# A Mamba-2 scan with a gated FFN on one Trainium2 core: the first chunk's scan in two units of 64 tokens, and the start-up in another order

## The chip, the core and the metric

The kernel runs on one core of a Trainium2 chip. The core has a matrix engine (TensorE, PE in the profile; PEld is its weight load), a vector engine (VectorE, DVE), an activation engine (ScalarE, ACT), a general engine (GpSimd, POOL) and a sequencer that issues transfers (SyncE, SP); each works through its own queue in order, and semaphores tie the queues together. Matrix products land in PSUM, everything else lies in SBUF, the inputs and the output in HBM. The metric is the device time of one execution in microseconds (us), the median of several runs; lower is better.

## The reference

Two parts are joined. The first is a state-space scan over four sequences, 8 heads, 768 tokens, 32 values a head and a state of 16; the second is an FFN of width 256 to 2048 to 256 on all 3072 tokens, with the gate h * cos(h). All data are fp32.

```python
log_a = np.log(np.clip(a, 1e-06, 1.0))
for c in range(nc):                        # the result does not depend on the chunk's length
    cum = np.cumsum(la, axis=-1)
    L = np.exp(cum[:, :, :, None] - cum[:, :, None, :]) * causal
    CB = np.einsum('bhin,bhjn->bhij', Cc, Bc)
    y_intra = np.einsum('bhij,bhjd->bhid', CB * L, xc)
    y_inter = np.einsum('bhin,bhnd->bhid', Cc, state) * np.exp(cum)[:, :, :, None]
    y[:, :, sl] = y_intra + y_inter
    Bx = np.einsum('bhjn,bhjd->bhjnd', Bc, xc) * decay_from_j[:, :, :, None, None]
    state = decay_full[:, :, None, None] * state + np.sum(Bx, axis=2)
# ... y as rows of tokens, heads side by side: x of (3072, 256)
h = x @ w_in
g = h * np.cos(h)
return g @ w_out
```

## The kernel before

The kernel cuts the 768 tokens into six chunks of 128 (NC = 6). A chunk's FFN is 16 steps (NF = 16); step n makes one PSUM bank of h (`first`), its cosine and gate, and two steps later adds to the output (`second`). The scan of chunk c + 1 is slipped in between the steps of chunk c. Only chunk 0 has no FFN before it to hide its scan behind. Its u is one of two halves of the tokens, and even and odd steps alternate between them:

```python
def turn_of(n):
    c, f = divmod(n, NF)
    return (f % 2, f // 2) if c == 0 else divmod(f, NJ)

def first(n):
    hp[n] = bank([P, TB], "hp", "h")           # two banks in turn
    for e in range(2):
        for k in range(KT):
            PE.matmul(to_[:, e], lhsT=w_in[:, k, fs], rhs=y[:, k, u], ...)
    ACT.activation(k, hp[n], AF.Copy, bias=0.25, scale=INV_2PI)
    V.scalar_tensor_tensor(out=w, in0=hp[n], scalar=INV_2PI, in1=k, ...)
```

Chunk 0's scan takes the four sequences one after the other, 128 tokens each. The decays between tokens j and i come from products of a: a is spread over partitions by a matmul (`spread_a`) and multiplied up by a running product on VectorE (`decays0`). The block from the second 64 tokens to the first 64 comes from another matmul (`cross`).

```python
def spread_a(b, tag):                          # 2 matmuls of 64x512
    for t in range(2):
        PE.matmul(ps[t * W:(t + 1) * W], lhsT=those[:, b:b + 1].to_broadcast([P, W]), rhs=a0s[:, t], ...)

def decays0(b):                                # one scan of 128x512, then GpSimd moves a half
    V.tensor_tensor_scan(out=l[:, 0]..., data0=spread.pop(b)..., data1=unit0..., ...)
    G.tensor_copy(out=l[W:P, 1], in_=l[W:P, 0])
    G.memset(l[W:P, 0], 0.0)

def turn(b, tag=None):                         # B and C of one sequence transposed, C cut in two
    for k in range(2):
        PE.transpose(tp[:, k], bc[:, k, heads(b)]..., ident)
    ...
def intra(b):                                  # g = C B^T, m = g * lam
    ...
def finish(b, tag, fills=0):                   # y = m x, and its copy to SBUF
    for h in range(H):
        PE.matmul(y[32 * q:32 * q + 32, t], lhsT=xr[:, b, h], rhs=m[:, :, h], ...)
    ACT.copy(out=yT[0][:, :, b * P:(b + 1) * P], in_=y[:, 0:2])
```

The weights of the FFN come in 16 pieces of 512 KB ("in" 0 to 7, "out" 0 to 7). They arrive as pairs of 32-bit words, and each piece is turned into fp32 by `grade` and `join`:

```python
def grade(which, i, later=False, n=1):
    ACT.activation(mags[e], high[e].bitcast(FP32), AF.Abs)
    G.tensor_scalar(out=mags[e], in0=mags[e], scalar1=MOST, scalar2=LEAST, ...)
    ACT.activation(lasts[e], low[e], AF.Copy, scale=2.0 ** -29)

def join(which, i):
    V.tensor_scalar(out=bits, in0=bits, scalar1=3, scalar2=0x3FFFFFFF, ...)
    V.scalar_tensor_tensor(out=bits, in0=high, scalar=0xC0000000, in1=bits, ...)
    G.tensor_tensor(out=dst.bitcast(U32), in0=bits, in1=last, op=ALU.add)
```

The start of the program, in the order in which each engine gets its instructions:

```python
fill(warm, 2)                                  # matmuls on ones, nobody reads them
spread_a(0, "h"); turn(0); spread_a(1, "h"); spread_a(2, "o"); spread_a(3, "h")
for b in range(NB):
    decays0(b)
turn(1, "h"); cross(0, "o"); intra(0); turn(2, "h"); cross(2, "o"); intra(1)
finish(0, "o"); grade("in", 0, n=2); intra(2); turn(3, "h"); finish(1, "o", 1)
# ... cut and la: all of a, clipped, written to HBM for the later chunks
join("in", 0); finish(2, "o"); intra(3)
grade("in", 1); rest = grade("out", 0, later=True); join("in", 1)
for n in range(NC * NF + LAG):
    first(n)
    if n == 0:
        first_scan()                           # finish(3), and the sums for the states
    # ... grade the next piece, gate(n), join, gated(n); from n = 2 on second(n - 2)
```

Of the kernel before, what the change touches and what calls it, by code (L numbers as in the profile page):

```python
# [25 lines left out]
def kernel(  # L26
# [10 lines left out]

# [54 lines left out]
    def load(c, seqs=(0, NB), only=(B, C, x)):  # L108
# [8 lines left out]
        for dst, src in ((bc[:, 0], B), (bc[:, 1], C), (xr, x))[::2 if c > 1 else 1]:  # L117
# [3 lines left out]
            halves = c > 0 and src is not C  # L121
# [9 lines left out]

    def by_blocks(c, u):
        return c > 1

    def load_blocks(c, u):


# [33 lines left out]
    a0 = const.tile([P, P], FP32, name="a0")  # L171
    a0z = const.tile([P, P], FP32, name="a0z")
    nc.sync.dma_start(out=a0[0:NB * H], in_=a[:, :, 0:P].rearrange("b h p -> (b h) p"))
    for r in (slice(NB * H, W), slice(W, P)):
        V.memset(a0[r], 1.0)
# [34 lines left out]

# [19 lines left out]
    def join(which, i):  # L230

        parts = held.pop((which, i), ())
        for e, (high, bits, last) in enumerate(parts):
# [12 lines left out]
    for b in range(NB):  # L248
        if b == NB - 1:
            fetch("in", 0)  # L250
        load(0, (b, b + 1))
    nc.sync.dma_start(
        out=a_in, in_=a.rearrange("(u b) h (c p) -> (b h c) u p", u=NU, p=P))
    for w in (("in", 1), ("out", 0), ("in", 2), ("out", 1), ("in", 3)):
        fetch(*w)
# [5 lines left out]
    V.memset(quarter, HALF_PI)  # L261


    unit = const.tile([P, HH * P + W], FP32, name="unit")
    G.tensor_copy(out=unit[:, 0:HH * P].rearrange("p (h i) -> p h i", h=HH),
                  in_=ident.unsqueeze(1).to_broadcast([P, HH, P]))


    ms = [scan.tile([P, 2 * H * W], FP32, tag=f"m{b}", bufs=1, name="m") for b in range(NB)]
    m_of = [t.rearrange("p (e h i) -> p e h i", e=2, h=H) for t in ms]  # L270
    m_at = [t.rearrange("p (h i) -> p h i", h=H) for t in ms]
    unit0, tos = m_of[NB - 1][:, 0], m_of[NB - 1][:, 1]
    for t in range(2):
        ts = slice(t * W, (t + 1) * W)
        V.tensor_copy(out=unit0[ts], in_=ident[ts, ts].unsqueeze(1).to_broadcast([W, H, W]))

    slot = const.tile([P, 2], FP32, name="slot")
# [7 lines left out]

    ACT.activation(const.tile([P, 1], FP32, name="sine"), quarter, AF.Sin)


    clip = dict(scalar1=1.0, scalar2=1e-6, op0=ALU.min, op1=ALU.max)
    G.tensor_scalar(out=a0z, in0=a0, **clip)  # L290
    G.memset(a0z[:, 0:P:W], 0.0)
    V.tensor_scalar(out=a0, in0=a0, **clip)


    to = const.tile([P, W], FP32, name="to")
    V.tensor_tensor_scan(out=to, data0=a0[:, W:P], data1=ones[:, 0:W], initial=1.0,
                         op0=ALU.mult, op1=ALU.mult)
    fro = const.tile([P, W], FP32, name="fro")
    V.memset(fro, 1.0)
    V.tensor_tensor_scan(out=fro[:, W - 2::-1], data0=a0[:, W - 1:0:-1],  # L300
                         data1=ones[:, 0:W - 1], initial=1.0, op0=ALU.mult, op1=ALU.mult)
    fros = const.tile([P, NB, W], FP32, name="fros")
    V.tensor_tensor(out=fros, in0=fro.unsqueeze(1).to_broadcast([P, NB, W]),
                    in1=those.unsqueeze(2).to_broadcast([P, NB, W]), op=ALU.mult)
    V.tensor_reduce(out=slot, in_=ident.rearrange("p (k t n) -> p t k n", t=2, n=N),
                    axis=mybir.AxisListType.XY, op=ALU.add)


    a0s = m_of[NB - 2]
    halves = a0z.rearrange("p (t i) -> p t i", t=2)  # L310
    for h in range(HH):
        ACT.activation(a0s[:, :, h], halves, AF.Copy, scale=mine[:, h:h + 1])
    for t in range(2):
        G.tensor_tensor(out=a0s[:, t, HH:H], in0=halves[:, t:t + 1].to_broadcast([P, HH, W]),
                        in1=mine[:, HH:H].unsqueeze(2).to_broadcast([P, HH, W]), op=ALU.mult)
    G.tensor_tensor(out=tos, in0=to.unsqueeze(1).to_broadcast([P, H, W]),
                    in1=mine.unsqueeze(2).to_broadcast([P, H, W]), op=ALU.mult)
# [6 lines left out]

    spread = {}

    def spread_a(b, tag):


        spread[b] = ps = bank([P, H, W], "a_ps", tag)  # L330
        for t in range(2):
            PE.matmul(ps[t * W:(t + 1) * W], lhsT=those[:, b:b + 1].to_broadcast([P, W]),
                      rhs=a0s[:, t], start=True, stop=True, tile_position=(0, t * W),
                      skip_group_check=True)

    def decays0(b):

        lam[0, b] = l = scan.tile([P, 2, H, W], FP32, tag="lam", bufs=4, name="lam")  # L340
        flat = "p h i -> p (h i)"
        V.tensor_tensor_scan(out=l[:, 0].rearrange(flat), data0=spread.pop(b).rearrange(flat),
                             data1=unit0.rearrange(flat), initial=0.0,
                             op0=ALU.mult, op1=ALU.add)
        G.tensor_copy(out=l[W:P, 1], in_=l[W:P, 0])
        G.memset(l[W:P, 0], 0.0)

    def cross(b, tag):

        ps = bank([P, H, W], "l_ps", tag)  # L350
        PE.matmul(ps, lhsT=fros[:, b:b + 2].rearrange("p b j -> p (b j)"), rhs=tos,
                  start=True, stop=True)
        for t in range(2):
            ACT.copy(out=lam[0, b + t][0:W, 1], in_=ps[t * W:(t + 1) * W])
            weigh(0, b + t)
# [31 lines left out]
    def turn(b, tag=None):  # L387
# [8 lines left out]
        for t in range(2):  # L396
            ACT.activation(cT[:, t], tp[:, 1], AF.Copy, scale=slot[:, t:t + 1])
# [517 lines left out]
```

## Time and profile before

| | before |
|---|---|
| time, median of 3 runs | 376.96 us (376.21 to 377.3) |
| span of the profiled execution | 374.9 us |
| first matmul of step 0 (hp, L578) | 17.81 us |
| first matmul of the second product (o, L637) | 25.71 us |
| one step of the FFN in chunk 0, hp and o | 3.46 us |
| last matmul ends | 371.2 us |

In the views, a line begins with a time from the start of the span, a length, the engine, the line of the kernel, the operation, and output <- inputs by their names; what stands in square brackets is the time for which the engine was idle just before, and who released it. A matmul in fp32 counts as two instructions (x8 for the four of one step). The granted clock of TensorE is 0.998 of full speed over the span. The two last microseconds after the last matmul are the last output's way to HBM.

### The profile page before, as it was taken

The numbers are of one execution on the slowest core, as the hardware profiler recorded it, in microseconds if no ns is written. First come the engines' busy times: TensorE is split into PE (matmuls) and PEld (weight loads), VectorE is DVE, ScalarE is ACT, GpSimd is POOL, SyncE is SP. The second block draws the span as 40 slices with busy tenths as digits, with TensorE's granted clock in tenths as the row PEclk, the third lists the DMA queues.
The fourth block names the chain that finished last, engine by engine and source line by source line (L and its number), as shares of the span: only waits on it lengthen the run. The fifth ranks groups of instructions, "written<-read, shape, count | busy, mean of one in ns | idle before, by whom it ended". The sixth has DMA issues, their size and how long they took to land.

```text
span 374.9 us, 8382 instructions
## 1 busy us (share of the span) xinstructions
PE 367.1 (98%) x3108; PEld 325.4 (87%) x3108; DVE 286.0 (76%) x478; ACT 176.0 (47%) x304; POOL 215.1 (57%) x335
## 2 busy tenths in 40 slices
PE   8999999999999999999999999999999999999996
PEld 3478888889899899999899998999999989999995
DVE  8879999889799957987767987766887872554543
ACT  3887666544344434344334445434444443443442
POOL 6767555589946346665354693353775344444451
PEclk9999999999999999999999999999999999999999
DMA  7989896514545741663322655121020000010011
GB/s 84 263 239 285 243 219 117 128 15 99 151 92 78 131 108 16 84 153 77 76 54 21 91 141 131 25 51 17 4 41 8 11 21 2 0 30 0 2 28 29
DMA packets 124424, 31.52 MB, mean 84 GB/s; under 512 B 93568, under 2 KB 120288, under 8 KB 124384
## 3 DMA queue, kind: packets, MB, share of 16 engines
q1 hardware_dynamic: 124224, 30.86, 38.4%
q8 instruction: 24, 0.39, 0.4%
q14 instruction: 16, 0.13, 0.1%
q10 hardware_dynamic: 160, 0.13, 0.1%
HBM read 27.64 MB, written 3.34 MB: 83 GB/s over the span
## 4 chain that ended last, share of the span: by engine, by line
PE 83%; SPq 5%; POOL 4%; DMA 3%; DVE 2%; issue 1%; ACT 1%; POOLq 0%; DVEq 0%; ACTq 0%
PE hp L578 40%; PE o L675 29%; PE o L637 7%; SPq L127 4%; PE y L516 3%; PE g L474 2%; DMA words<-in_moe_w_in_dram 1%; POOL words L613 1%; PE y L509 1%; POOL gd L619 1%; DMA bc<-in_B_dram 1%; DMA blocks<-in_C_dram 1%; POOL gd L622 1%; PE o L720 1%; PE s_ps L537 0%
## 5 line engine op out<-in xcount | busy, mean ns | idle before, releaser
L578 PE MATMUL hp<-yT,w_in 128*128 128x256 f32 x768 | 183.7, 382 | 1.9 <-DVE gT L594 1.4
L578 PEld LDWEIGHTS hp<-yT,w_in 128*128 128x128 f32 x768 | 139.4, 190 | 21.6 <-issue 2.0
L619 POOL TENSOR_TENSOR gd<-gT 128x256 f32<-128x256 f32 x79 | 59.2, 750 | 100.0 <-DVE gT L594 91.2
L589 ACT ACTIVATE w<-w,quarter 128x512 f32<-128x512 f32 x96 | 69.2, 721 | 76.8 <-DVE w L584 76.7
L582 ACT ACTIVATE k<-hp 128x512 int32<-128x512 f32 x96 | 57.2, 595 | 82.3 <-PE hp L578 82.0
L584 DVE SCALAR_TENSOR_TENSOR w<-hp,k 128x512 f32<-128x512 f32 x96 | 65.4, 681 | 37.3 <-ACT k L582 37.1
L594 DVE TENSOR_TENSOR gT<-hp,w 128x512 f32<-128x512 f32 x96 | 65.2, 679 | 34.6 <-ACT w L589 24.8
L675 PE MATMUL o<-words,gd 128*128 128x128 f32 x474 | 65.9, 275 | 0.0
L675 PEld LDWEIGHTS o<-words,gd 128*128 128x128 f32 x474 | 59.3, 192 | 0.1
L378 DVE TENSOR_TENSOR_SCAN lam<-arow,unit 128x512 f32<-128x512 f32 x40 | 57.0, 1426 | 0.0
L675 PEld LDWEIGHTS o<-w_out,gT 128*128 128x128 f32 x316 | 47.5, 191 | 4.0
L622 POOL TENSOR_TENSOR gd<-gT,gd 128x128 f32<-128x128 f32 x79 | 45.5, 577 | 6.2
L675 PE MATMUL o<-w_out,gT 128*128 128x128 f32 x316 | 48.0, 274 | 0.0
L621 POOL TENSOR_TENSOR gd<-gT,gd 128x128 f32<-128x128 f32 x79 | 44.2, 560 | 6.2
L495 DVE TENSOR_TENSOR m<-g,lam 128x256 f32<-128x256 f32 x80 | 30.9, 415 | 0.5
L637 PE MATMUL o<-w_out,gT 128*128 128x256 f32 x128 | 30.3, 380 | 0.4 <-POOL w_out L246 0.4
L675 PE MATMUL o<-w_out,gd 128*128 128x128 f32 x158 | 30.6, 275 | 0.0
L675 PE MATMUL o<-words,gT 128*128 128x128 f32 x158 | 30.6, 275 | 0.0
L637 PEld LDWEIGHTS o<-w_out,gT 128*128 128x128 f32 x128 | 24.2, 190 | 4.0 <-POOL w_out L246 0.8
L675 PEld LDWEIGHTS o<-words,gT 128*128 128x128 f32 x158 | 24.0, 192 | 0.0
L675 PEld LDWEIGHTS o<-w_out,gd 128*128 128x128 f32 x158 | 24.0, 192 | 0.0
L692 DVE TENSOR_TENSOR sum<-ps,sum 128x256 f32<-128x256 f32 (+1 forms) x27 | 16.7, 644 | 0.6
(98 smaller groups left out, 274.5 us busy)
## 6 DMA issues: line engine op xcount, KB each, us to landing
arow<-a_cut SPq DMA_DIRECT2D x20, 512.0 KB
words<-in_moe_w_in_dram SPq DMA_DIRECT2D x8, 512.0 KB
words<-in_moe_w_out_dram SPq DMA_DIRECT2D x8, 512.0 KB
out_dram<-sum SPq DMA_DIRECT2D x18, 128.0 KB
blocks<-in_B_dram SPq DMA_DIRECT2D x128, 8.0 KB
blocks<-in_C_dram SPq DMA_DIRECT2D x128, 8.0 KB
xr<-in_x_dram SPq DMA_DIRECT2D x14, 128.0 KB
along<-a_all SPq DMA_DIRECT2D x20, 64.0 KB
```

The lines of the kernel that those rows point to most:

```text
L378: V.tensor_tensor_scan(out=lam[c, b][:, hs].rearrange("p h i -> p (h i)"), data0=rows_.rearrange("p h i -> p (h i)"), data1=unit[:, b % 2 ...
L495: V.tensor_tensor(out=m_[js, :, :, is_], in0=g_[js, :, :, is_], in1=l_[js, :, :, is_], op=ALU.mult)
L578: PE.matmul(to_[:, e], lhsT=w_in[:, k, fs], rhs=y[:, k, u], start=(k == 0), stop=(k == KT - 1), skip_group_check=True)
L582: ACT.activation(k, hp[n], AF.Copy, bias=0.25, scale=INV_2PI)
L584: V.scalar_tensor_tensor(out=w, in0=hp[n], scalar=INV_2PI, in1=k, op0=ALU.mult, op1=ALU.subtract)
L589: ACT.activation(cos, cos, AF.Sin, bias=quarter, scale=TWO_PI)
L594: V.tensor_tensor(out=gT[n], in0=hp.pop(n), in1=cos, op=ALU.mult)
L619: G.tensor_tensor(out=d[:, 0:2], in0=g[:, 1:2].to_broadcast([P, 2, P]), in1=g[:, 3::-3], op=ALU.subtract)
L621: G.tensor_tensor(out=d[:, 2], in0=g[:, 0], in1=d[:, 0], op=ALU.subtract)
L622: G.tensor_tensor(out=d[:, 3], in0=g[:, 2], in1=d[:, 2], op=ALU.subtract)
L637: PE.matmul(o[c, u][:, t], lhsT=g[:, 2 * e + t], rhs=w_out[:, 2 * j + e], start=(j == e == t == 0), stop=(j == NJ - 1 and e == 1), skip_gr ...
L675: PE.matmul(at[q], lhsT=a_[q], rhs=w[q], start=(j == 0 and q in starts), stop=(j == NJ - 1), skip_group_check=True)
```

## The change

Chunk 0's scan is done in two units. Unit k holds tokens 64k to 64k + 63 of all four sequences: two sequences side by side on the 128 partitions (s), two pairs (p). Unit 0 needs no cross block and no state before it. Unit 1 gets the state that unit 0 leaves, as later chunks do (`reach0`, `weigh_c`, the first matmuls of `finish0`). The purpose is that step 0 of the FFN needs unit 0 only, so that it can start before the rest of the chunk is scanned; unit 1's scan then lies inside step 0. In chunk 0 the FFN's u is the unit, so even steps take unit 0 and odd steps unit 1.

With it the order of step 0 on all engines is written out in a function of its own, and the transfers are reordered: a, B, C (on ScalarE's queue) and the first weight piece before x, then unit 1's data. The constants are made by other engines; the identity pattern that later chunks need is written in step 0 over the one that chunk 0 uses.

```diff
-    for b in range(NB):
-        if b == NB - 1:
-            fetch("in", 0)
-        load(0, (b, b + 1))
+    load_bc(0, (0,))
+    load_bc(0, (1,), nc.scalar)
+    fetch("in", 0)
+    load_x(0)
+    load_bc(1)
+    fetch("in", 1)
+    load_x(1)
     nc.sync.dma_start(
         out=a_in, in_=a.rearrange("(u b) h (c p) -> (b h c) u p", u=NU, p=P))
-    for w in (("in", 1), ("out", 0), ("in", 2), ("out", 1), ("in", 3)):
+    for w in (("out", 0), ("in", 2), ("out", 1), ("in", 3), ("out", 2), ("in", 4)):
         fetch(*w)
 ...
+    share_a(0, G, 6, H)
+    share_a(0, V, 0, 6)
+    share_a(1, G, 0, H)
 ...
+    def turn0(k, tps, which=(0, 1)):
+        for w in which:
+            of = tps[0][:, 0:2] if w == 0 else tps[-1][:, -2:]
+            for p in range(2):
+                PE.transpose(of[:, p], bcs[k][:, w, p]..., ident)
+            for t in range(2 * w):
+                ACT.activation(cuts[k][:, :, t], of, AF.Copy, scale=slot[:, t:t + 1])
+            if k or w == 0:
+                ACT.copy(out=turns0[k][:, w], in_=of)
 ...
+    def inner(k):                      # 16 matmuls of 32x64 on 128 columns
+    def weights(k, q):                 # m = g * lam, one of two halves
+    def finish0(k):
+        y = [pair("y") for _ in range(2)] if k else [pair("y")]
+        if k:
+            ...                        # 16 matmuls: state of unit 0 with rT
+        ...                            # 32 matmuls of 64 columns: y = m x
+        ...                            # 16 matmuls into the same tile y[0]: the state's sums
+        ...                            # ACT copies y to yT (one copy, or two for k = 1)
+        for t in range(2):
+            ACT.activation(new[:, :, :, ts], y[0]..., AF.Copy, scale=slot[:, t:t + 1])
+        if k == 0:
+            return
+        for s in range(2):
+            G.tensor_tensor(out=dec[:, s], in0=old[:, s], in1=r4[:, s, :, W:]..., op=ALU.mult)
+        G.tensor_tensor(out=new, in0=new, in1=dec, op=ALU.add)
 ...
-    ...                                # the old order, shown above
+    fill(bank([P, 4, P], "warm", "o"), 1)
+    fill(bank([P, 2, P], "warm", "o"), 1)
+    spread_a(0, 0)
+    decays0(0, 0)
+    turn0(0, [bank([P, 2, P], "tp", "o")], (0,))
+    spread_a(0, 1)
+    decays0(0, 1)
+    turn0(0, [bank([P, 2, P], "tp", "o")], (1,))
+    grade("in", 0, n=2)
+    weigh0(0)
+    inner(0)
+    for q in range(2):
+        weights(0, q)
+    for p in range(2):
+        spread_a(1, p, "o")
+    join("in", 0)
+    finish0(0)
+    decays0(1, 0)
+    decays0(1, 1)
+    reach0(1)
 ...
+    def first_step():
+        first(0, lambda: turn0(1, ...))   # the transposes between hp(0)'s halves
+        weigh0(1)
+        weigh_c(1)
+        inner(1)
+        fill(bank([P, 4, P], "warm", "o"), 1)
+        for q in range(2):
+            weights(1, q)
+        wind(0)                        # k and w of step 0
+        grade("in", 1)
+        clips()                        # cut, la and the identity pattern
+        join("in", 1)
+        gate(0)
+        finish0(1)
+        grade("out", 0)
+        gated(0)
+        rest = grade(*piece[1], later=True)
+        join("out", 0)
+        rest()
+    first_step()
     rest_of_loads()
-    for n in range(NC * NF + LAG):
+    for n in range(1, NC * NF + LAG):
 ...
-        (ACT.copy if u else V.tensor_copy)(out=ob, in_=o[c, u])
-        for s in range(2):
-            nc.sync.dma_start(out=to_rows[2 * u + s, c], in_=ob[s * W:(s + 1) * W])
+        ACT.copy(out=ob, in_=o[c, u])
+        for p in range(2):
+            nc.sync.dma_start(out=unit_rows[p, u], in_=ob[p * W:(p + 1) * W])
```

## The prediction, made before the changed kernel had run

> **What bounds the kernel now.** I read the page's busy shares first, then the busy time in stretches, then the chain of waits in its first 32 us, then the timeline of TensorE over the same time.
>
> ```profile
> PE 367.1 (98%) x3108; PEld 325.4 (87%) x3108; DVE 286.0 (76%) x478; ACT 176.0 (47%) x304; POOL 215.1 (57%) x335
> 0.00:25.00 25.00, 23.25 (x186) 12.01 (x186) 20.70 (x37) 17.12 (x41) 17.07 (x37) 1.00 0.91 206
> 25.00:50.00 25.00, 24.58 (x115) 21.40 (x114) 23.69 (x35) 18.05 (x30) 16.65 (x18) 1.00 0.85 227
> 300.00:350.00 50.00, 49.95 (x436) 46.17 (x435) 25.05 (x42) 22.24 (x37) 23.57 (x43) 1.00 0.04 9
> ```
>
> The columns of a stretch are its limits and length, then the busy time of PE, PEld, DVE, ACT and POOL. TensorE is busy everywhere, but weight loads fill only 12.01 of the first 25 us against 46.17 of 50 late on: before 25 us the busy PE carries small scan matmuls, fills and slow warm-up, and everything after is matmuls back to back. So the end time is the moment from which PE no longer waits, plus a fixed amount of work.
>
> ```profile
> 12.29 5.41 DMA words<-in_moe_w_in_dram
> ...
> 18.42 0.58 ACT last L220
> 19.00 0.62 POOL mag L223
> ...
> 21.18 1.28 POOL w_in L246
> 22.46 0.59 POOL mag L223
> ...
> 23.09 0.43 DVE mag L236
> ...
> 23.54 0.70 DVE mag L238
> ...
> 24.38 1.28 POOL w_out L246
> ...
> 25.71 1.99 PE o L637 x8
> ```
>
> That is the chain (start, length, what). It does not run through the scan. It runs through the preparation of the FFN weights, "grade" (ACT, POOL) and "join" (DVE, POOL), and its last link releases the first matmul of the second product, o(0), at 25.71.
>
> ```profile
> 17.81 2.29 PE L578 MATMUL hp<-yT,w_in 128*128 128x256 f32 x8 [0.33 <-POOL w_in L246]
> 20.03 0.65 PE L424 MATMUL y<-m,xr 128*32 128x128 f32 x16
> 20.49 0.63 PE L537 MATMUL s_ps<-xr,sc 128*32 128x64 f32 x32
> 21.16 1.99 PE L578 MATMUL hp<-yT,w_in 128*128 128x256 f32 x8
> 23.32 1.97 PE L578 MATMUL hp<-yT,w_in 128*128 128x256 f32 x8 [0.16 <-DVE gT L594]
> 25.71 1.99 PE L637 MATMUL o<-w_out,gT 128*128 128x256 f32 x8 [0.42 <-POOL w_out L246]
> ```
>
> hp(0) starts at 17.81, hp(1) at 21.16, hp(2) at 23.32. From 25.71 on both kernels have the same PE work (hp(3), o(1), ... and five scans), and the waits of PE after it are four of 0.5 to 0.6 us. So I have to find one number: when o(0) starts in the changed kernel.
>
> [...] here the four 512-column warm passes took 0.93 us each (3.71/4), against 0.43 in steady state (two times 0.216, a 256-column pass). [...]
>
> **The change part by part.** Chunk 0 used four batches of 128 tokens, all finished before or just after hp(0). Now unit 0 holds tokens 0 to 63 of all four sequences, unit 1 tokens 64 to 127. hp(0) needs unit 0 only, and unit 1's scan is put inside step 0. I lay the queues out by hand, with durations of like rows.
>
> Until a0 is spread: ones at 1.0, fills now 2 passes of 512 and 2 of 256 columns, 2x0.93 + 2x0.46 = 2.8, so to 3.85. a0's data is seen at 2.63 as before, clip 0.23, and share_a in two shares on DVE (384 columns, about 0.4) and POOL (128 columns, 0.4)[...]: 3.75. Spread of one half costs 4 passes, two at a time, 0.9 warm (2.79/3)[...]: 3.85 to 5.4.
>
> The old start had 16 spread passes and four scans of 1.2 us in row (5.98 to 10.78). The new unit 0 has two: 5.4 to 6.6 and 6.6 to 7.8. Transposes of B and C (0.35 each) and the second spread fill PE to 6.95; ACT cuts C twice (0.67) to 7.65; 32 passes of inner at 0.02 to 0.025 us (the chunk-1 row: 32 in 0.81) to 8.45; weights two times 0.61 on DVE to 9.75.
>
> PE meanwhile does both spreads of unit 1 (1.75) to 10.2, then y: 64 passes of 64 columns at 0.014 to 0.02 (s_ps, the same size, ran 32 in 0.45), 0.95, and 32 of the state, 0.45: 11.6. The copy of y to SBUF reads the same tile as the state's products, so I let it wait for both: 0.6, so 12.25. The weights: words are the fourth transfer on SP's queue instead of the eleventh. Before, some 9,000 small packets had landed by 9 us; B, C and x of unit 0 are about 6,100, so the piece lands near 7. ACT, POOL, DVE and POOL then have its first half ready at 11.6. hp(0) starts at 12.3, 5.5 us sooner than 17.81.
>
> Step 0 gives much of it back. First half of hp(0) to 13.15, transposes of B, 13.5; ACT copies, 13.9; transposes of C to 14.3, because they share a tile with B; second half of hp(0) to 15.1. DVE has the join (2.1 as in the old one), two scans and the reach scan behind it, 9.75 + 2.15 + 2.4 + 0.65 = 14.95. ACT cuts and copies C to 15.35; inner to 16.05; weights 16.1 to 17.35. finish0(1) reuses the banks of both g tiles, so it starts there: state part 0.5, y 0.95, sum 0.45: 19.3. Two copies of 0.35: 20.05. hp(1) starts at 20.1, 1.1 us sooner than before.
>
> Then hp(1) and hp(2), 1.75 each, end at 23.6; w_in piece 1 is joined at 20.7, early enough. In an ideal case o(0) begins there: 25.71 - 23.6 = 2.1 us gained. But o(0) needs w_out piece 0. POOL and ACT have first to do unit 1's ends: ACT copies y and two state parts (to 20.65), then grades "out 0" (0.6): 21.25. POOL has the clips (1.85), the join of piece 1 (1.28, to 20.7), two decay products (0.42 each) and the sum of states (0.65): 22.2. Then mag 0.62, 22.85; it goes straight on to the mag of the next piece[...]; DVE 0.3 + 0.69: 24.4; POOL 1.28: 25.7. So o(0) begins at 25.75, practically where it was, and PE is idle for about 2 us before it instead of about 0.5.
>
> The sum is then: hp(0) -5.5, hp(1) -1.1, o(0) from -2.1 (no wait for w_out) through 0 (my layout) to +2. Moved output rows, one copy moved from DVE to ACT and the later place of chunk 1's transfers lie behind PE: chunk 1's first decays are only due four steps (14 us) later. I count them as 0, with 0.5 us either way for the four later waits.
>
> **The rivals.** First: the w_out chain is shorter than I have it, and PE runs through. For it: the new order of step 0 must have been meant for this[...]. Against: from 16.5 to 25.7 POOL has only two gaps in my layout, 0.5 and 0.95 us. It would give 374.8 to 375.5. Second: the small matmuls, 64 passes where there were 32 of twice the width, are held by issue or weight loads at 0.03 us rather than 0.015 (the old y matmuls of 128 columns took 0.03). Then y and sum of both units cost 2 x 1.4 us more, unit 1's end and POOL's state sum come later, and o(0) starts near 27.5: 378.8. Third: B arrives later than it is wanted at 5.4. 4,096 packets of 64 bytes for B and C are needed where 2,048 were; the trace moved 1,000 a us in the 3rd and 4th us and 1,400 later, so B lands between 4.9 and 6. C from ACT's queue may help the start, or only share the same engines. Cost 0 to 0.6 us, all passed on to the end.
>
> **Range and chances.** My layout gives +0.05, so 377.0. My errors are one-sided toward caution (I have waited at every shared tile), and the order was evidently arranged around these very waits, so I go 0.6 below: 376.4. The first rival sets the lower end, 374.4, with 0.4 us below it for an earlier scan; the second, with part of the third, the upper end, 378.7. Two per cent is 7.5 us. The faster side would need the whole of hp(0)'s 5.5 us kept and 2 more; the slower side a stall of 7 us, several times each rival. So faster 0.01, same 0.97, slower 0.02.
>
> **What would show it right or wrong.** Right: hp(0) starts at 12 to 13, hp(1) near 20, PE waits 1 to 2 us for w_out from POOL ahead of o(0) near 25.7, and the rest of the trace is the old one shifted. If the first wait of PE in step 0 is for a scan or a transfer, or y's 64 passes take over 1.5 us, the second or third rival has it. The prediction is wrong if o(0) starts before 23.5 or after 28, or if a wait of over 1 us that was not there comes up after 30 us.

## The result, and the profile after

The changed kernel took 379.68 us (378.28 to 380.11) against 376.93 us for the kernel before in the same series: a ratio of 1.0065, with a 95% interval of 1.0039 to 1.0091. The prediction was 376.4 with a range of 374.4 to 378.7, so the measured time lies above the range, and the change made the kernel slower by 2.75 us. The span of the profiled execution grew from 374.9 to 377.5 us.

First the page's busy shares and the busy time in stretches of the changed kernel (limits, length, then PE, PEld, DVE, ACT, POOL, clock, DMA share, GB/s):

```profile
PE 364.9 (97%) x3266; PEld 325.1 (86%) x3266; DVE 280.8 (74%) x469; ACT 172.8 (46%) x295; POOL 211.9 (56%) x336
0.00:25.00 25.00, 21.23 (x344) 11.78 (x344) 14.50 (x29) 13.11 (x30) 15.89 (x37) 1.00 0.88 208
25.00:50.00 25.00, 22.49 (x104) 19.82 (x105) 23.51 (x34) 17.25 (x29) 15.70 (x17) 1.00 0.87 216
300.00:350.00 50.00, 49.95 (x436) 46.20 (x435) 26.47 (x47) 21.07 (x34) 22.99 (x43) 1.00 0.05 12
```

Every engine has less to do, and TensorE's busy time fell by 2.2 us. But more of TensorE's time is idle early on: 3.8 us of the first 25 where it was 1.75, and 2.5 of the next 25 where it was 0.4. From 300 us on TensorE is as busy as before (49.95 of 50 us). The timeline of TensorE shows where it stands still (in brackets the idle time before a line, and who ended it):

```profile
3.92 1.87 PE L333 MATMUL a_ps<-m,those 128*64 128x512 f32 x4
6.16 0.41 PE L360 MATMUL tp<-ident,bc 128*128 128x128 f32 x2 [0.38 <-DMA bc<-in_B_dram]
11.37 0.80 PE L422 MATMUL y<-m,xr 64*32 64x64 f32 x60
13.41 1.10 PE L634 MATMUL hp<-yT,w_in 128*128 128x256 f32 x4 [0.23 <-ACT yT L442]
15.25 0.44 PE L360 MATMUL tp<-ident,bc 128*128 128x128 f32 x2 [0.52 <-ACT turned L364]
21.28 3.72 PE L634 MATMUL hp<-yT,w_in 128*128 128x256 f32 x16 [0.46 <-ACT yT L440]
27.51 1.99 PE L697 MATMUL o<-w_out,gT 128*128 128x256 f32 x8 [2.51 <-POOL w_out L251]
```

hp(0) starts at 13.41 (before 17.81), hp(1) at 21.28 (before 21.16), o(0) at 27.51 (before 25.71), after a wait of 2.51 us for w_out. The chain of waits (start, length, what) has changed its character:

```profile
2.01 4.01 DMA bc<-in_B_dram
...
6.57 1.01 PE a_ps L333 x4
...
13.41 1.10 PE hp L634 x4
...
16.88 0.50 ACT k L641
17.38 0.58 ACT mag L227
...
18.04 0.61 POOL mag L228
18.65 0.55 POOL unit L814
...
19.46 0.69 POOL cut L817
...
21.03 1.05 POOL w_in L251
...
22.26 0.77 POOL whole L455 x2
...
23.10 0.73 POOL state L457
...
23.91 0.62 POOL mag L228
...
24.56 0.83 DVE mag L241
...
25.42 0.70 DVE mag L243
...
26.19 1.27 POOL w_out L251
...
27.51 1.99 PE o L697 x8
```

Before, the chain began with the transfer of the weights' words, and the scan was not on it. Now it begins with the transfer of B, runs through unit 0's scan, hp(0) and unit 1's transposes, and only then enters the weights, in single file and for the most part on GpSimd: grade of w_in 1, the identity pattern, the clips, join of w_in 1, unit 1's state sum, grade of w_out 0, join of w_out 0. Scan and weights, which had run side by side, stand one behind the other.

Of the 2.6 us in the span, 1.8 are there when o(0) starts. From o(0) to the start of the last o it is 343.93 us instead of 343.52, another 0.4. The waits of TensorE after 28 us (us in total, times, the longest):

```profile
PE hp L634 <- DVE gT L653: 1.2, 2, 0.6
PE g L531 <- ACT cT L515: 0.5, 1, 0.5
```

The first is as long in the kernel before (1.2 us, two times). The second, near 185 us, is new: chunk 3's blocks of C land later. The chains of the two kernels, before and then after, have their last transfer as

```profile
180.17 2.01 DMA blocks<-in_C_dram
```

```profile
181.84 2.55 DMA blocks<-in_C_dram
```

SyncE starts these transfers at 180.06 instead of 178.39, which is no more than all of TensorE's work there is late (hp of that step: 181.95 instead of 180.16). What makes the wait is that the one that ends it takes 2.55 us from issue to landing instead of 2.01; why, these two profiles do not show. The last o (L780) starts at 371.44, where before it was 369.23. The remaining 0.4 us is on the last output's way out: from the end of the last matmul to the end of the span it is 4.1 us instead of 3.7 (3.7, not the two microseconds that the text ahead speaks of).

### The profile page after: what moved, and what is told of

It is laid out like the page before. It is cut to its first block, busy times and chain, and to the rows that moved or that the text cites. A ratio compares the mean times of both kernels' runs of the same rounds, so it can differ in the third digit from the quotient of the medians.

```text
span 377.5 us, 8675 instructions
## 1 busy us (share of the span) xinstructions
PE 364.9 (97%) x3266; PEld 325.1 (86%) x3266; DVE 280.8 (74%) x469; ACT 172.8 (46%) x295; POOL 211.9 (56%) x336
## 4 chain that ended last, share of the span: by engine, by line
PE 71%; DVE 11%; POOL 8%; issue 4%; ACT 2%; DMA 2%; SPq 1%; DVEq 0%; POOLq 0%; ACTq 0%
PE hp L634 34%; PE o L735 29%; POOL words L672 3%; PE y L573 2%; DVE mag L243 2%; DVE w L643 2%; DVE gT L653 2%; DVE mag L241 1%; PE g L531 1%; PE y L566 1%; DVE lam L481 1%; DMA bc<-in_B_dram 1%; POOL gd L678 1%; PE o L697 1%; PE a_ps L333 1%
## 5 line engine op out<-in xcount | busy, mean ns | idle before, releaser
L680 POOL TENSOR_TENSOR gd<-gT,gd 128x128 f32<-128x128 f32 x79 | 44.1, 558 | 6.2
L681 POOL TENSOR_TENSOR gd<-gT,gd 128x128 f32<-128x128 f32 x79 | 42.6, 539 | 6.2
```

The lines of the kernel that those rows point to most:

```text
L680: G.tensor_tensor(out=d[:, 2], in0=g[:, 0], in1=d[:, 0], op=ALU.subtract)
L681: G.tensor_tensor(out=d[:, 3], in0=g[:, 2], in1=d[:, 2], op=ALU.subtract)
```

## The experiments

The theory after this comparison: the end is set by the order of step 0's queues (w_out 0 stands behind unit 1's work on GpSimd), and about 1 us comes from unit 0's late start. The rivals: the wait is only the last of many, so that taking it away moves it elsewhere; and, after the first runs, that idle time on TensorE costs a second time, through its clock. Ratios are to the kernel before in the same series, with the 95% interval; they take in the runs as a whole, so a few long ones can move a ratio where the median stays. o(0) and its wait are from the one profile of each kernel; "low clock" counts the timed runs whose mean clock was below 0.9965 (nearly all of them at about 0.995).

| run | median us | ratio | o(0) starts, wait | low clock |
|---|---|---|---|---|
| changed kernel | 379.68 | 1.0065 [1.0039, 1.0091] | 27.51, 2.51 | 2 of 4 |
| w_out_first | 378.72 | 1.0053 [1.0034, 1.0071] | 24.96, none | 1 of 6 |
| b_two_queues | 377.89 | 1.0042 [1.0026, 1.0058] | 26.69, 2.67 | 6 of 22 |
| two_tiles | 378.51 | 1.0056 [1.0028, 1.0084] | 30.07, 2.68 | 5 of 12 |
| clips_last | 383.63 | 1.0208 [1.0171, 1.0245] | 27.14, 2.14 | 5 of 6 |
| weights_ahead | 377.53 | 1.0028 [1.0014, 1.0042] | 25.68, none | 0 of 22 |
| b_and_tiles | 378.29 | 1.0028 [1.0013, 1.0043] | 27.15, 2.69 | 11 of 22 |
| weights_b_tiles | 377.48 | 1.0008 [0.9996, 1.0020] | 24.78, 0.22 | 12 of 23 |
| weights_b_tiles_warm | 377.73 | 1.0027 [1.0011, 1.0042] | 26.70, none | 12 of 22 |
| gap_filled | 378.71 | 1.0061 [1.0040, 1.0082] | 27.56, filled | 1 of 11 |
| b_tiles_gap_filled | 377.77 | 1.0020 [1.0004, 1.0035] | 26.92, filled | 1 of 22 |
| weights_b_tiles_early_blocks | 377.35 | 1.0010 [1.0001, 1.0020] | 24.86, none | 10 of 22 |
| before_w_out_late | 379.88 | 1.0076 [1.0059, 1.0093] | 29.07, 2.91 | 4 of 6 |
| reordered_act_unit | 376.37 | 0.9969 [0.9956, 0.9982] | 23.86, 0.55 | 0 of 22 |
| reordered_late_unit | 377.03 | 0.9995 [0.9985, 1.0006] | 24.51, 0.54 | 1 of 22 |

**w_out_first** puts w_out 0 ahead of the whole end of unit 1 (its y, the copies and the state sum), and the identity pattern behind it.

```diff
         grade("in", 1)
-        clips()                         # with the identity pattern
+        grade("out", 0)
+        clips()                         # without it
         join("in", 1)
         gate(0)
-        finish0(1)
-        grade("out", 0)
         gated(0)
-        rest = grade(*piece[1], later=True)
         join("out", 0)
+        finish0(1)
+        unit_again()
+        rest = grade(*piece[1], later=True)
         rest()
```

> The changed kernel, with the first w_out piece prepared before unit 1's ends: its grade follows that of w_in piece 1, its join stands ahead of the copies and state products of unit 1, and of the clips only the two products are left ahead of the joins. Theory (the chain that ends last is the preparation of w_out piece 0, queued on ScalarE and GpSimd behind unit 1's last operations): o(0) starts when hp(2) ends, near 25.0 us instead of 27.51, the wait of 2.5 us is gone, and the time falls by 2.3 to 2.6 us, to about 377.2 (ratio to before 1.000). Rival (unit 1's scan itself sets the end, through the late start of unit 0): hp(1) and hp(2) stay the bound, o(0) moves by under 0.8 us, the time stays above 378.8.

Measured: o(0) has no wait and starts at 24.96, 2.55 us sooner. But two steps later TensorE stands still for nearly as long, and the time is 378.72 us, not the 377.2 expected (timeline of TensorE in this run):

```profile
24.96 1.99 PE L697 MATMUL o<-w_out,gT 128*128 128x256 f32 x8
32.84 3.49 PE L634 MATMUL hp<-yT,w_in 128*128 128x256 f32 x8 [2.43 <-DVE gT L653]
```

In that run's chain, w_in 2 now waits behind the state sum (25.70) and the identity pattern (26.38 to 27.16) on GpSimd, VectorE's join of it behind that, and the gate of step 2 behind the join. So the cause of the wait was right, and taking it away alone moves it: GpSimd has 3.4 us of state sum, identity pattern and clips to place (by their times in the changed kernel's chain), and in both orders a part of it stands ahead of a weight piece on the path. Besides, the eight instructions of hp(4) take 3.49 us instead of 1.9: from 32.51 to 35.93 us the granted clock is 0.50, see below.

**b_two_queues** splits both B and C of unit 0 over SyncE's and ScalarE's queues; in the changed kernel B was on one and C on the other.

```diff
-    load_bc(0, (0,))
-    load_bc(0, (1,), nc.scalar)
+    load_bc(0, engs=(nc.sync, nc.scalar))     # one sequence of a pair each
```

> The changed kernel, with B and C of unit 0 each issued half by SyncE and half by ScalarE, B first on both. Theory of the late start (B lands at 6.02 us, 0.4 us after TensorE wants it, because C shares the engines from the start): B lands before 5.5, the transposes start when the first spread ends (5.8 us or earlier), and the whole chain behind moves 0.3 to 0.4 us forward, to 379.3. Rival (the cold clock in the first spread, not B, sets the start): the wait for B goes, but lam is made at the same time and the end moves by less than 0.2 us.

Measured, in its timeline of TensorE:

```profile
3.92 1.30 PE L332 MATMUL a_ps<-m,those 128*64 128x512 f32 x4
5.15 0.44 PE L359 MATMUL tp<-ident,bc 128*128 128x128 f32 x2
12.43 1.10 PE L633 MATMUL hp<-yT,w_in 128*128 128x256 f32 x4
26.69 1.99 PE L696 MATMUL o<-w_out,gT 128*128 128x256 f32 x8 [2.67 <-POOL w_out L251]
```

The transposes of B no longer wait, and hp(0) and o(0) come 0.98 and 0.82 us sooner. Unit 0's start is thus on the path, and most of what it gains is passed on to o(0). About 0.4 us of it is B's wait, and 0.57 that the first spread took 1.30 us and not 1.87; the second part is more likely the warm-up of this run (full clock first at 4.4 us, in the changed kernel's profile at 5.55) than the edit. SyncE's issue of one of these transfers takes 0.76 us in the changed kernel's chain, so that one issue less ahead of B's second half is enough for the 0.4 us (an estimate from these two figures). That C shares the transfer engines with B from the start fits the changed kernel's profile too: from 2 to 4 us the packets of ScalarE's queue, which are C's, took 65.6% of the time of 16 engines, and those of SyncE's, B's among them, 36.9%.

**two_tiles** gives unit 1's transposes of B and of C a tile each, so that the second does not wait for the copy of the first.

```diff
-        first(0, lambda: turn0(1, [pair("tp")[:, 0]...]))
+        first(0, lambda: turn0(1, [pair("tp")[:, 0]... for _ in range(2)]))
```

> The changed kernel, with the transposes of unit 1's B and C in two PSUM tiles instead of one. Theory (a false dependency inside the tile holds C's transposes until B has been copied): the wait of 0.52 us in step 0 goes, C is cut 0.6 us earlier, inner(1) starts near 16.1 instead of 16.67, and since ScalarE's queue behind it is on the chain, o(0) comes 0.4 to 0.6 us earlier: 379.2. Rival (w_out's chain is bound elsewhere, by GpSimd's own work): the wait goes and o(0) stays within 0.2 us.

Measured: the wait of 0.52 us is gone, and from hp(0) to hp(1) it is 7.19 us instead of 7.87. In the profiled run full clock is first recorded at 13.9 us (both first spreads took 1.98 us, hp(0) started at 16.48), so that its times can only be compared from hp(0) on: o(0) comes 13.59 us behind it instead of 14.10. The 0.5 us is thus passed on, as expected; the rival had o(0) stay.

**clips_last** moves the clips and the identity pattern behind w_out 0.

```diff
         grade("in", 1)
-        clips()
         join("in", 1)
 ...
         join("out", 0)
+        clips()
         rest()
```

> The changed kernel, with all of the clips (two copies, two products, one memset on GpSimd, 2.4 us) moved behind the join of w_out piece 0. Theory (GpSimd's queue as a whole is the bound from 18 to 27.5 us): o(0) comes 1.5 to 2 us earlier, near 25.7, 377.9. Rival (the queue waits for VectorE and ScalarE, and the clips lie in its gaps; only 0.3 us of them reach the join of w_in piece 1): o(0) gains 0.3 us, and the transfers of chunk 1, which wait for the clips, start 6 us later, which may add a new wait near 40 us: 379.4 to 381.

Measured: o(0) comes only 0.37 us sooner, still after a wait of 2.14 us: the 2.1 us that the clips and the pattern take on GpSimd were not simply added to the path, since the chain through VectorE and the joins is nearly as long (in this run's chain VectorE's products and join come ahead of GpSimd's join of w_in 1, which starts at 20.77 instead of 21.03). After 28 us the waits of TensorE grew to 1.8 us for gates (three waits) and 1.6 us for the blocks of C. The time of 383.63 goes further than these (the one profiled run has a span of 379.1 and full clock, the others a mean clock down to 0.986); where the other runs lost it no profile shows.

**weights_ahead** is w_out_first with the grade of w_in 2 also ahead of unit 1's end. **weights_b_tiles** adds b_two_queues and two_tiles to it, **weights_b_tiles_warm** one more fill during C's cut, and **b_and_tiles** has the two edits of unit 0 and 1 without any change of order.

```diff
         gate(0)
+        in2 = grade("in", 2, later=True)
         gated(0)
         join("out", 0)
         finish0(1)
+        in2()
         unit_again()
-        rest = grade(*piece[1], later=True)
-        rest()
```

> As w_out_first (w_out piece 0 prepared before unit 1's ends), and also the grade of w_in piece 2 moved ahead of unit 1's state products and of the two copies of the identity pattern. In w_out_first the wait of 2.5 us only moved from o(0) to hp(4), where the gate of step 2 stood on VectorE behind the join of a piece that GpSimd reached too late. Theory (the order of the weight pieces in the queues is the whole of it): o(0) near 25.0, hp(4) no later than 30.5, no wait over 0.5 us before 50 us, no drop of the clock there: 377.2, the time of before. Rival (the start is short of GpSimd or VectorE time, whatever the order): the wait moves on to a later step and the time stays at 378.5 or more.

> weights_ahead together with b_two_queues and two_tiles. Theory (PE is then the bound, and what the scan gains reaches the end): hp(1) near 19.6, o(0) near 23.3, about 1.6 us before weights_ahead: 375.5 in runs without a drop of the clock, ratio 0.996 to before. Rival (weight transfers or preparation come next): o(0) or hp(4) waits again, and the time is 376.5 to 377.5.

> The same with one more fill (256 columns) in the gap of 0.9 us in which TensorE waits for the cut C of unit 0. Theory of the clock (idle gaps in the first 10 us and at o(0) let the clock stay or fall to half in some runs, which costs about 2 us there): the runs lie closer together than without the fill, fewer than one in six is more than 1.5 us above the lowest; the median as in weights_b_tiles or up to 0.5 us lower. Rival (the drop has to do only with the long wait in front of o(0) and hp(4)): no difference from weights_b_tiles.

> b_two_queues and two_tiles together, weights in the order of the changed kernel. Theory (the weights' queue is serial behind unit 1's scan, so what the scan gains is passed on in full): o(0) near 26.0, 1.5 us before the changed kernel's 27.51, still with a wait of 2.5 us for w_out; 377.2 where the clock holds, about 379.5 where it drops. Rival (w_out is bound by GpSimd's own work): o(0) stays at 26.7, as in b_two_queues.

Measured: each removed wait shows in the start of o(0) (25.68 for weights_ahead against 27.51 in the changed kernel, 24.78 for weights_b_tiles against 27.15 for b_and_tiles). But the expected times were missed: the medians come no lower than 377.48 where 377.2 and 375.5 were expected, and in both kernels hp(4) still waits 1.3 us for the gate of step 2, as the rival of weights_b_tiles had it. The extra fill of weights_b_tiles_warm did not draw the runs together: 6 of 22 are over 1.5 us above the lowest. The runs of one kernel fall into groups. Of b_and_tiles' 22 runs 11 have a mean clock of 0.995 and a median of 378.9; the other 11 have 376.9, which is where the kernel before is. (Not every long run is of this kind: weights_ahead has three of 380.4 to 380.7 with a mean clock of 1.0, and no profile shows what held them up.) The profile of b_and_tiles shows what lies behind its groups. The busy time in three stretches of 3.41 us, laid on a grid that begins where the trace first records full clock (6.85 us in this run; columns as above, the clock third from the end):

```profile
23.92:27.33 3.41, 0.72 (x4) 0.32 (x3) 2.31 (x4) 1.81 (x4) 2.32 (x4) 1.00 0.96 233
27.33:30.75 3.42, 3.42 (x9) 2.71 (x10) 3.35 (x6) 2.63 (x5) 2.13 (x3) 0.50 0.72 159
30.75:34.16 3.41, 3.41 (x18) 3.00 (x17) 2.32 (x4) 1.43 (x4) 1.83 (x3) 1.00 1.01 344
```

TensorE was busy for 0.72 of 3.41 us, idle for 2.69, and the clock is at half for the next 3.41 us (27.33 to 30.75): 9 matmul instructions instead of 18. The same grid laid over the other runs, first weights_b_tiles_warm, then w_out_first, then b_two_queues, then the changed kernel, the stretch with the wait and the one after it:

```profile
18.80:22.21 3.41, 1.63 (x87) 1.39 (x68) 2.22 (x4) 3.41 (x9) 2.41 (x5) 1.00 1.03 380
22.21:25.62 3.41, 3.41 (x10) 2.69 (x9) 1.55 (x2) 1.61 (x3) 3.33 (x5) 0.50 1.07 345
```

```profile
29.10:32.51 3.41, 1.31 (x7) 0.80 (x5) 3.38 (x5) 2.33 (x4) 2.35 (x3) 1.00 0.93 235
32.51:35.93 3.42, 3.09 (x7) 2.52 (x8) 2.80 (x5) 1.30 (x2) 2.79 (x3) 0.50 1.08 383
```

```profile
24.89:28.31 3.42, 1.62 (x8) 1.44 (x9) 2.60 (x5) 2.36 (x4) 1.85 (x2) 1.00 0.76 134
28.31:31.72 3.41, 3.41 (x17) 3.02 (x16) 3.38 (x6) 2.47 (x4) 2.59 (x3) 1.00 0.68 184
```

```profile
22.61:26.03 3.42, 2.39 (x12) 1.75 (x10) 1.44 (x3) 2.70 (x5) 2.33 (x5) 1.00 1.06 351
26.03:29.44 3.41, 1.93 (x9) 1.73 (x10) 2.59 (x6) 2.36 (x4) 1.95 (x3) 1.00 0.69 100
```

Idle times of 1.78, 2.10 and 2.69 us in one stretch are followed by half clock; idle times of 1.80 and 1.48 are not, although the wait itself was as long (2.67 and 2.51 us): on this grid it lay across a border. Six of the 16 profiles have such a half-clock stretch while TensorE still has work; it begins 5, 5, 6, 7, 8 and 53 lengths of the grid after the first full clock, and the stretch ahead of it has 1.78 to 2.69 us of idle time. Of the stretches with full clock behind them only that of b_two_queues has as much. In these profiles the line thus lies near 1.8 us in 3.41, and where a wait of 2.5 us falls on the grid changes from profile to profile (full clock first appears between 4.2 and 6.9 us in all profiles but that of two_tiles). This would give one kernel two groups of runs, as seen. The next runs test it.

**gap_filled** and **b_tiles_gap_filled** put two fills (matmuls on ones that nobody reads) into TensorE's wait, in the changed kernel and in b_and_tiles.

```diff
+        if n == LAG:
+            fill(bank([P, 4, P], "warm", "o"), 2)
         if n >= LAG:
             second(n - LAG)
```

> The changed kernel with two fills (512 columns each, about 0.9 us each) put on TensorE ahead of o(0), where it was idle for 2.5 us. The path is not touched: o(0) still waits for GpSimd's add of w_out and starts at 27 to 27.8. If the clock theory holds (a 3.41 us window, counted from the warm-up, with about 1.8 us or more of idle in it, gives the next window half the clock), the runs with a mean clock of 0.995 (2 of 4 in the changed kernel) become rare (under 1 in 5) and the median falls from 379.7 to about 378.4. If the half clock has another cause, their share stays at a half and the median stays near 379.7.

> b_and_tiles (11 of 22 runs at a mean clock of 0.995, medians 378.9 for those and 376.9 for the others) with the same two fills ahead of o(0). Clock theory: nearly all runs in the upper group of the clock, median 377.0, o(0) still near 27. Rival: half of the runs stay at 0.995 and the median stays at 378.3.

Measured: o(0) starts where it did (27.56, and 26.92 against 27.15), and the low clock is gone: 1 of 11 instead of 2 of 4, and 1 of 22 instead of 11 of 22. The same work with the same wait, only not idle, keeps the clock; the rival, another cause for the half clock, falls by the 22 runs of b_tiles_gap_filled (the changed kernel's four runs alone would be too few). For b_tiles_gap_filled the busy time in the stretch of the wait is now 2.51 us:

```profile
23.31:26.72 3.41, 2.51 (x9) 1.11 (x7) 2.12 (x3) 1.83 (x4) 2.32 (x3) 1.00 1.08 291
26.72:30.14 3.42, 3.42 (x16) 2.90 (x16) 3.24 (x5) 2.63 (x6) 2.13 (x4) 1.00 0.43 73
```

The expected 377.0 was missed: the median is 377.77, only 0.5 under that of b_and_tiles, and the intervals of the two ratios overlap. For gap_filled the ratio, 1.0061, is no better than the changed kernel's 1.0065. So the fills show no gain in time that is clear of noise, and most of the changed kernel's loss is there without half clock. The median of b_and_tiles' runs at full clock was the wrong yardstick. They are not a fair sample, since what spares them the half clock may also bring the full clock early; that was not tried by itself.

**before_w_out_late** delays w_out 0 in the kernel before, with no other change.

```diff
             G.tensor_tensor(out=dst.bitcast(U32), in0=bits, in1=last, op=ALU.add)
+            for _ in range(3 if (which, i) == ("out", 0) else 0):
+                G.tensor_scalar(out=dst, in0=dst, scalar1=1.0, scalar2=1.0, ...)
```

> The kernel before with three extra GpSimd products by 1.0 (0.62 us each) on w_out piece 0 behind its add: the result is the same, o(0) comes 1.9 us later (27.5, as in the changed kernel), behind a gap of about 2.3 us on TensorE. If the start of o(0) alone sets the end, the whole delay arrives: 378.8 in runs at full clock, and by the clock theory a part of the runs (a fifth to a half) is at 0.995 and 1.7 longer. If there is slack behind o(0), the time stays under 377.9; if idle does not touch the clock, no run is at 0.995.

Measured: 2.95 us slower, with 4 of 6 runs at low clock, where the kernel before had 0 of 33, 1 of 75, 1 of 48 and 2 of 43 in the four series. Two runs at full clock took 379.3 and 379.6, that is 2.5 us more. The delay was meant to be 1.9 us, but in the profile the three products take 2.40 us and TensorE's wait grows from 0.42 to 2.91, so it arrives whole. In that profile hp(0) was late as well (18.58 instead of 17.81), so o(0) starts only at 29.07, and the clock dropped after it:

```profile
26.93:30.35 3.42, 1.28 (x6) 1.16 (x7) 2.98 (x6) 2.12 (x5) 3.17 (x5) 1.00 0.93 218
30.35:33.76 3.41, 3.41 (x10) 2.70 (x9) 2.66 (x4) 0.31 (x1) 2.62 (x3) 0.50 0.98 336
```

So a late o(0) behind an idle TensorE is enough to make the old kernel as slow as the changed one. No slack shows behind o(0), and the split scan isn't needed for such a loss.

**weights_b_tiles_early_blocks** starts the later chunks' block transfers one step earlier.

```diff
-    block_loads = {NF * (c - 1) - 9 + 8 * u: ...
+    block_loads = {NF * (c - 1) - 10 + 8 * u: ...
```

> weights_b_tiles (12 of 23 runs at 0.995, median 377.5; in the profiled run the half clock came right after a wait of 1.6 us for chunk 3's blocks of C) with the block transfers one step earlier in SyncE's queue. If these waits are what is left, the wait near 185 us is gone, the 0.995 runs fall to under 1 in 5 and the median is 376.5 to 376.9, under the kernel before by 0.1 to 0.5. If SyncE's queue is simply behind and the order does not matter, the wait stays and so do median and share.

Measured: in weights_b_tiles TensorE waits 1.6 us for the blocks of C, is idle for 2.10 us of the 3.41 up to 187.27 us, and has half clock (0.50) from there to 190.69 us:

```profile
PE g L530 <- ACT cT L514: 1.6, 1, 1.6
```

With the earlier transfers the wait is gone; the waits of TensorE after 100 us are one line in this run:

```profile
PE hp L633 <- DVE gT L652: 0.6, 1, 0.6
```

Still, 10 of 22 runs are at low clock, and the median is 377.35. The expectation of fewer than 1 in 5 failed: this profile has another wait of 1.8 us, for unit 1's y ahead of hp(1), and one of 1.3 us ahead of hp(4). In its timelines ScalarE stands before w_out's words until 18.46, with the gate and unit 1's y queued behind, and GpSimd copies the identity pattern (26.28 to 27.7) ahead of w_in 2.

**reordered_act_unit** and **reordered_late_unit** resolve these two. ScalarE does the gate ahead of w_out's grade; w_out's join and the next grade stand between unit 1's copies and its state sum; the clips fill GpSimd's wait ahead of w_in 1; and the identity pattern goes to ScalarE, or to GpSimd at the end of step 2.

```diff
         grade("in", 1)
-        grade("out", 0)
         clips()
-        join("in", 1)
         gate(0)
-        in2 = grade("in", 2, later=True)
+        join("in", 1)
+        out0 = grade("out", 0, later=True)
         gated(0)
-        join("out", 0)
-        finish0(1)
+        def between():                  # called between the copies and the state sum of finish0
+            out0()
+            join("out", 0)
+            return grade("in", 2, later=True)
+        in2 = finish0(1, between)
         in2()
         unit_again()                    # by ACT; or by GpSimd behind step 2
```

> weights_b_tiles_early_blocks in a further order: the clips ahead of w_out's grade and the gate ahead of it on ScalarE, w_out's last cut, join and the next grade between unit 1's copies and its state sum, and the identity pattern copied by ScalarE instead of GpSimd. Theory (the order of the queues in step 0 alone holds the gain back): hp(1) waits under 0.6 us (there 1.8), o(0) starts at 23.7 to 24.5, hp(4) waits under 0.7 us (there 1.3), few runs at 0.995, median 375.3 to 376.4, below before. Rival (the words of w_out land too late, or ScalarE becomes the bound): a wait of 1 us or more stays ahead of hp(1), o(0) or hp(4), and the median stays at 377 or above.

> As reordered_act_unit, but the identity pattern is copied by GpSimd at the end of step 2 (1.4 us of its time, when the first pieces are through) and ScalarE is free of it. If ScalarE's two copies (about 1 us) delay k(1) and the chain behind it, this one is the faster by 0.2 to 0.6 us; if GpSimd's copies push a later piece, its o(2) or hp(5) waits and it is slower by as much.

Measured for reordered_act_unit, timeline of TensorE:

```profile
19.59 3.72 PE L635 MATMUL hp<-yT,w_in 128*128 128x256 f32 x16 [0.46 <-ACT yT L439]
23.86 0.48 PE L698 MATMUL o<-w_out,gT 128*128 128x256 f32 x1 [0.55 <-POOL w_out L251]
24.92 1.78 PE L698 MATMUL o<-w_out,gT 128*128 128x256 f32 x7 [0.58 <-issue]
30.61 1.97 PE L635 MATMUL hp<-yT,w_in 128*128 128x256 f32 x8 [0.46 <-DVE gT L654]
```

o(0) starts at 23.86, no wait is over 0.6 us once step 0 has begun, no run is at low clock, and the kernel takes 376.37 us, at the edge of the 375.3 to 376.4 expected: less than the kernel before, by 0.18 to 0.44%. With GpSimd's copy in step 2 the wait ahead of hp(4) is 1.03 us, and the gain is gone (0.9995).

So with everything moved at once the split does gain. The order of the queues in step 0 is a part of it, but not all: this kernel also has B and C on two queues, a tile for each transpose, earlier block transfers, and the identity pattern's copies (0.7 to 1.5 us on GpSimd in the other profiles) moved to ScalarE. The new order with the copy still on GpSimd has a ratio of 0.9995 where weights_b_tiles_early_blocks had 1.0010 in another series, and only ScalarE's copy brings it to 0.9969.

Over all these kernels the share of runs at low clock goes with the longest wait of TensorE in the profile once step 0 has begun. Where it is 1.3 us or less (the kernel before, weights_ahead and the two reordered kernels) it is at most 2 of 43. Where it is 1.6 us or more and not filled, it lies between 1 of 6 and 5 of 6.

## Why the prediction was wrong

**Right: the kind of limit.** The prediction had o(0) set by w_out from GpSimd, behind the clips, the join of w_in 1 and unit 1's sums, with TensorE idle for about 2 us. It is that very chain, and the wait is 2.51 us. From hp(0) to hp(1) it had 7.8 us; measured 7.87, in part by luck: unit 1's products end 7.41 us behind hp(0) instead of 7.0, and from there hp(1) waits 0.46 us for the copies instead of 0.8. The second rival (small products at 0.03 us) is refuted: 60 of them in 0.80 us. That its figures, o(0) near 27.5 and 378.8 us, came close to the measured ones is luck, since its cause was not there. Of the prediction's own signs, those of being wrong did not come up (o(0) started before 28, and no wait of over 1 us came after 30 us), but those of being right did not either: hp(0) at 12 to 13, hp(1) near 20, o(0) near 25.7. What failed are terms of the sum.

**Mis-sized: "hp(0) starts at 12.3".** It started at 13.41. In the layout the first spread takes 1.55 us (0.9 from its row of the trace, the rest its author's estimate for the slow start) and B is there when it ends; measured were 1.87 us, with full clock first recorded at 5.55 us, and 0.38 us of wait (the third rival). The second spread with the transposes took 1.79 us instead of 1.55, and the cuts of C up to `inner` 0.93 instead of 0.70. Most of such a delay is passed on to o(0), as the prediction said of the third rival: in b_two_queues hp(0) is 0.98 us sooner, o(0) 0.82. The path was right and the costs on it were too small; the late B stood among the rivals and not in the sum. The split itself put the scan onto the chain.

**Mis-sized: "so o(0) begins at 25.75".** From hp(1) to o(0) the layout has 5.65 us, measured 6.23. GpSimd ends the join of w_in 1 at 22.08 instead of 20.7, 0.2 more than hp(1)'s delay explains, the sums at 23.83 instead of 22.2, and w_out at 27.46 instead of 25.7. The 0.6 us from 22.85 to 23.45, in which the layout has VectorE's shift (L241) stand behind GpSimd's next mag, were its author's estimate: in the changed kernel's profile the shift starts at 24.56, 0.02 us behind the mag that it needs, and takes 0.83 us, where at 19.47 and 28.11 it takes 0.42. Together with the 1.1 us of the start this makes the 1.8 us by which o(0) is later than 25.75.

**Failed: "I count them as 0, with 0.5 us either way".** This term stood for everything behind o(0). Measured are 0.4 us from o(0) to the last o, with the new wait of 0.5 us for the blocks of C in it, and 0.4 us at the end. (The "four later waits" are three in the views of the kernel before, of 0.6, 0.6 and 0.5 us; the fourth is o(0)'s own 0.42.) In two of the four runs the mean clock of 0.995 fits a stretch of 3.41 us at half clock on top (half of 3.41 us is 0.0045 of 377.5); no profile of the changed kernel shows it. The prediction had put no price on 2 us of idle TensorE beyond the 2 us. b_and_tiles and b_tiles_gap_filled show that such idle time can bring half clock (11 of 22 runs, and 1 of 22 when it is filled); how much of the changed kernel's time this is stays open.

**Failed: "so I go 0.6 below".** The correction rested on the order having been arranged around these waits, not on a row of the profile. reordered_act_unit shows that the order was not the best one, and that the first rival is not reached even so: with another order, two queues for B and C, more tiles and less work on GpSimd, 376.37 us, or 0.87 under the median of the kernel before in its series, where the first rival had 1.5 to 2.1.

Of the 3.3 us between 376.4 and 379.68 the late o(0) is 1.8, what lies behind it 0.8, and this correction 0.6.

## What to carry to other kernels

When work is taken off the start of a kernel, write the queue of each engine from the new start on and see which chains that ran side by side now share one engine in order; the gain arrives only when the last of them is moved, and each removed wait can show the next. Look at the long waits of TensorE, and at the granted clock behind them: here, where the longest was 1.6 us or more and not filled, 1 of 6 to 5 of 6 of the runs were at low clock, and where it was 1.3 us or less at most 2 of 43. A fill of unread products took that away (from 11 of 22 runs to 1 of 22), but showed no gain in time clear of noise. Compare groups of runs at the same clock only with care, for what sets the clock may also set the start.

## What the runs showed of the hardware

Six profiles have half clock (0.50) while TensorE still has work, each for one stretch of 3.41 us. In the 3.41 us just ahead of it TensorE was idle for 1.78 us (weights_b_tiles_warm), 2.10 (w_out_first, weights_b_tiles), 2.14 (before_w_out_late), 2.52 (two_tiles) and 2.69 (b_and_tiles). On the grid counted from the first full clock, full clock stayed behind stretches with 1.80 us of idle time (b_two_queues), 1.75 (weights_b_tiles_early_blocks), 1.62 (weights_ahead) and less.

Full clock was first recorded between 4.2 and 6.9 us (4.93 in the kernel before, 5.55 in the changed one), and in two_tiles' profiled run at 13.9 us. There TensorE was idle for 0.41 us from 3.65 to 7.07 us and for 0.93 us from 7.07 to 10.48. In every profile the 3.41 us ahead of the first full clock have at most 0.24 us of idle time (the most in weights_ahead). hp(0) came 3 us later in two_tiles than in the changed kernel (16.48 against 13.41).
